# One engine issues every transfer: SyncE's transfers put into the program's own order in a gated mix of sliding-window attention and a GELU block

## The chip, the cores and the metric

The kernel runs on one core of a Trainium2 chip. A core has a matrix engine (TensorE; PE in the profile, with its weight loads listed apart as PEld), a vector engine (VectorE, DVE), a scalar engine (ScalarE, ACT), a general engine (GpSimd, POOL) and an engine that here does nothing but issue transfers (SyncE, SP). Each works through its own list of instructions from first to last; between engines there are semaphores. Transfers between the chip's memory and the on-chip memory are moved by 16 DMA engines. The metric is the device time of one execution in microseconds (us), the median of several runs.

## The reference

For x of 2048 tokens by 512, in fp32:

```python
g = sigmoid((x * gate_w).sum(-1, keepdims=True))
q, k, v = split(x @ wqkv)            # 32 heads of 16, per head 2048 x 16
scores = q k^T / 4, kept where 0 <= i - j < 256, else -1e9
a = softmax(scores) v @ wo
b = gelu(x @ w1 + b1) @ w2 + b2      # 512 -> 1792 -> 512
out = g * a + (1 - g) * b
```

## The kernel before, in words

**Dense work.** All large products (qkv, the two of the GELU block, and wo) are made from pairs: every fp32 operand is split into a high part and a low remainder, and one product is three matmuls (`mm3`, lines 92 to 95) of 128x128 weights on 128x512 moving data. Tokens are cut into four tiles of 512 (`T`). `dense()` is one long generator: `qkv(t)` for the four tiles, then eight turns `mlp(n)` over `TURNS` (half of the 1792 columns for one tile of tokens: first the "u" products and the GELU, then the "y" products), then `final(t)`, the product with wo and the mix.

**Attention.** Heads are taken in eight groups of four (`g_`), keys in 16 blocks of 128. For each block `att_max` multiplies queries by keys on a "dense" layout (tiles `qd` and `kd`, result `sm`, line 446) to find each row's maximum on VectorE; twelve blocks later (`LEAD`) `att_exp` makes the scores on another layout (`qs`, `ks`, result `st`, line 490), ScalarE takes the exponential and GpSimd cuts the window; `att_pvs` multiplies with the values in `vbuf` (line 527). q, k and v were written to device memory by `qkv` and are read back by `load_qd`, `load_kd`, `load_qs`, `load_ks` and `att_load_v`. A group's stretch of 512 tokens is one "slot", four blocks long, and `qd`, `kd`, `ks` have two slots: the next stretch is loaded while the present one is used, and it can't be written before the last products on the slot's old content have been made.

**What sets the order.** The main loop runs over blocks; in each of the four quarters of a block it emits the attention's products and then `fill`s in a share (`STEP / 4`, or `STEP0 / 4` for the first twelve) of the dense generator's matmuls. `START` is how much dense work is done before attention begins. Work of the other engines is put off by `after(ns, fn)` against a clock of the program's own, which counts matmuls; `tick` runs what has come due, and `need` runs events until a condition is met. The engines listed in `MANUAL` take their instructions in exactly the order in which this emits them. SyncE is not in that list before: its transfers are ordered by the framework's scheduler, which may move them past one another. In the built program all 749 transfers are on SyncE; eight semaphores are used in turn, so a transfer waits for the landing of the eighth before it.

**Around the change.** At the end of a block with `m % NB == (u >= 0)`, that is after the second block of each stretch, `load_qd` and `load_kd` ask for the next stretch. At the end of a turn's "u" products `load_x` asks for the next tile's x, four transfers of 512 KB (line 590), into the one buffer `xt`. `load` brings weights at a pace (`PACE`), and `split` cuts them into halves `LAND` later. `ya_load` fetches the addend of the "y" products. `att_norm` divides: it loads the denominators (565), writes the reciprocals back (570), loads numerators and spread reciprocals (575), multiplies and stores (580).

Of the kernel before, what the change touches and what calls it, by code (L numbers as in the profile page):

```python
# [32 lines left out]
def gated_mix(ctx: ExitStack, tc: tile.TileContext, x, wqkv, wo, w1, b1, w2, b2, gate_w, out):  # L33
# [11 lines left out]
    def f32(ap):  # L45
        return ap.bitcast(F32)
# [98 lines left out]
            nc.sync.dma_start(raw.rearrange("p (c f) -> p c f", c=NC) if len(src.shape) == 3 else raw, src)  # L145
        raws[key] = raw

    def split(key, eng):

        kind, i = key  # L150
        raw = raws.pop(key)
        w = sb.tile([128, 2, T], F32R, tag="w", bufs=14, name=f"{kind}_{i}")
        nc.scalar.activation(w[:, 0], raw, AF.Copy)
        wt[key] = w.rearrange("p s (c f) -> p s c f", c=NC) if kind in ("qk", "w1") else w

        def lo():
            eng.tensor_sub(w[:, 1], raw, f32(w[:, 0]))
            done.add(("w", key))
        after(700, lo)

    paced = [0.0]

    def load(key):

        paced[0] = max(now[0], paced[0] + PACE)
        after(paced[0] - now[0], load_now, key)

    def load_now(key):
        load_raw(key)
        after(LAND, split, key, nc.vector)  # L170

# [78 lines left out]
    def qkv_qk(t, j):  # L250

        xt = xts[t]
        dst, i = (SQ[t], j) if j < NC else (SK[t], j - NC)
        w = wt["qk", j]
        p = ps.tile([128, T], F32, tag="d", bufs=2, name=f"qk{t}_{j}")
        for c in range(NC):
            mm3(p, w[:, 0, c], w[:, 1, c], xt[:, c, 0], xt[:, c, 1], c == 0, c == NC - 1)
            yield MM3
        e = sb.tile([128, 2, T], F32R, tag="h", bufs=7, name=f"qke{t}_{j}")

        h = 1 if j < NC else 0

        def hi():
            nc.scalar.activation(e[:, h], p, AF.Copy)  # L264

        def lo():
            nc.vector.tensor_sub(e[:, 1 - h], p, f32(e[:, h]))  # L267

        def store():
            to = dst[:, :, :, i].rearrange("h d s c -> (h d) s c")  # L270
            nc.sync.dma_start(to[:, 0:2], f32(e))
            nc.sync.dma_start(to[:, 2], f32(e[:, h]))
            done.add(("qk", t, j))
        after(100, hi), after(700, lo), after(700 + HOLD, store)

    def qkv_v(t, b):
        xt = xts[t]
        p = ps.tile([128, D], F32, tag="d", bufs=2, name=f"v{t}_{b}")
        ts = slice(b * 128, (b + 1) * 128)
        for c in range(NC):  # L280
            w = wt["v", c]
            mm3(p, xt[:, c, 0, ts], xt[:, c, 1, ts], w[:, 0], w[:, 1], c == 0, c == NC - 1)
            yield MM3
        vx = f32(sb.tile([128, 2, T], F32R, tag="h", bufs=7, name=f"vx{t}_{b}"))
        vx = vx.rearrange("p s t -> p (s t)")[:, 0:H * 17].rearrange("p (h c) -> p h c", c=17)
        nc.gpsimd.memset(vx[:, :, 16:17], 1.0)

        def ev():
            to = vx[:, :, 0:16].rearrange("p (s i g a) d -> p i s g a d", i=2, s=2, a=2)
            by = p.rearrange("p (i a g s d) -> p i s g a d", i=2, a=2, s=2, d=16)  # L290
            for i in range(2):
                for s in range(2):
                    nc.scalar.activation(to[:, i, s], by[:, i, s], AF.Copy)
            after(HOLD, store)
# [17 lines left out]
    def qkv(t):  # L312
# [4 lines left out]
        if t == 0:  # L317
            keys = qk + [("v", c) for c in range(NC)]
            load_xr(0)
            for key in keys[0:4]:  # L320
                load_raw(key, True)
            warm(WARM[0])
            for b in range(NB):
                qkv_x(0, b)
            warm(WARM[1])
            split(keys[0], nc.vector)
            split(keys[1], nc.vector)
            nc.sync.dma_start(gwb, gate_w.partition_broadcast(128))
        need(*[("x", t, b) for b in range(NB)])
        for n, (kind, j) in enumerate(pieces):  # L330
            if not last and XAT <= n < XAT + NC:
                nc.sync.dma_start(XT[t][n - XAT], f32(xts[t][:, n - XAT]))
            if kind == "qk":
                need(("w", (kind, j)))
            else:
                need(*[("w", ("v", c)) for c in range(NC)])
            if t == 0 and n < 4:
                load_raw(keys[n + 4], True)
                load_raw(keys[n + 8], True)
            if t == 0 and n == 10:  # L340
                nc.sync.dma_start(b1c, b1.rearrange("(f p) -> p f", p=128))
            if kind == "qk":
                yield from qkv_qk(t, j)
            else:
                yield from qkv_v(t, j)
            if t == 1 and n % 3 == 2:
                clear_k(n // 3)
            if t == 2 and n < 4:
                clear_q(n)
            if t == 2 and n in (1, 2):  # L350
                load_kd(0, n - 1)
            if t == 2 and n in (8, 9):
                load_ks(0, n - 8)
            if t == 0:
                for i in ([2], [3], [4], [5], [6], [7, 8], [9, 10], [11])[n] if n < 8 else []:
                    split(keys[i], nc.vector if i % 2 else nc.gpsimd)
                if n == 1:
                    gate(0)
                    load_xr(1)
            elif n == 0 and not last:  # L360
                load_xr(t + 1)
            if last and n not in (6, 7):
                load(later.pop(0))
            if last and n == len(pieces) - 1:
# [196 lines left out]
    def att_norm(t, c):  # L561
# [5 lines left out]

        def rcp():
            nc.vector.reciprocal(den, den)
            nc.sync.dma_start(RD[t][c].rearrange("h (j c) -> (h j) c", c=32), den)  # L570

        def back():
# [4 lines left out]
        def mul():  # L577
            num, rb = tiles
            nc.vector.tensor_mul(num, num, rb)
            nc.sync.dma_start(OT[t][c], num)  # L580
            done.add(("o", t, c))
        after(6000, rcp), after(10500, back), after(17000, mul)


    w1k = w1.rearrange("(c p) f -> p c f", p=128)

    def load_x(t, name):
        xt = sb.tile([128, NC, 2, T], F32R, tag="xt", bufs=1, name=f"{name}{t}")
        for c in range(NC):
            nc.sync.dma_start(f32(xt[:, c]), XT[t][c])  # L590
        xts[t] = xt

    def load_o(t, cs=range(NC)):
# [58 lines left out]
    def ya_load(k):  # L652
# [7 lines left out]
        else:  # L660
            need(("y", 0, t, b))
            nc.sync.dma_start(ya, YA[t][slice(b * 128, (b + 1) * 128)])

    ybs = {}

    def mlp(n):
        half, t = TURNS[n]
        if n == 0:
            ya_load(0), ya_load(1)
        last = n % NT == NT - 1  # L670
        xt = xts[t]
        hs = []
        for i in range(HF):
# [13 lines left out]
            for c in range(NC):  # L687
                nc.sync.dma_start(XT[t][c], f32(xt[:, c]))
        if n + 1 < len(TURNS) and TURNS[n + 1][1] != t:
            load_x(TURNS[n + 1][1], f"mx{half}")  # L690
        ps_ = {}

        def y_start(b):
# [4 lines left out]
        def y_end(b):  # L698
# [7 lines left out]
            nc.vector.scalar_tensor_tensor(y, ps_[b], 0.5, yas.pop(n * NB + b), op0=ALU.mult, op1=ALU.add)  # L706
            ya_load(n * NB + b + 2)

            def store():
                nc.sync.dma_start((YA, YB)[half][t][ts], y)  # L710
# [40 lines left out]
    def final(t):  # L751
# [3 lines left out]
        for b in range(NB):  # L755
# [8 lines left out]
            for k in range(n):  # L764
# [8 lines left out]
                def ev(p=p, nb=nb, a=a, cs=cs):  # L773
                    need(("yb", nb))
                    nc.vector.scalar_tensor_tensor(a[:, cs], p, g[:, nb:nb + 1], a[:, cs],
                                                   op0=ALU.mult, op1=ALU.add)
                    nc.sync.dma_start(out[nb * 128:(nb + 1) * 128, cs], a[:, cs])
                after(100, ev)


    later = [("w1", i) for i in range(HF)] + [("w2", i) for i in range(HF)]
# [32 lines left out]
    for u in range(-LEAD, NU):  # L814
        m = u + LEAD
        gm, bm = divmod(m, NKB)
        step = STEP if u >= 0 else STEP0
        for i in range(4):
            for op in ORDER:
                if op == "s" and u >= 0:  # L820
                    att_exp(u // NKB, u % NKB, i)
# [9 lines left out]
            load_qs(0, m - QAT)  # L831
        if m == QAT + NT:
            load_qs(0, NT - 1)
        if m % NB == (u >= 0) and NB <= m < NU - NB:
            load_qd(*divmod(m // NB + 1, NT)), load_kd(*divmod(m // NB + 1, NT))
        if u % NB == 0 and NB <= u < NU - NB:
            load_ks(*divmod(u // NB + 1, NT))
        if u % NB == 2 and NB < u < NU - 3 * NB:
# [8 lines left out]
    tick(1e9)  # L847


MANUAL = {mybir.EngineType.PE, mybir.EngineType.Activation, mybir.EngineType.DVE, mybir.EngineType.Pool}  # L850
MM3 = 3 * 227
LASTN = 2
WARM = (7, 3)
RB = 4
NKB = S // 128
PTS = 14
RAWS = 122e3
PUT = 1200
LEAD = 12
QAT = 5  # L860
START = 90e3
NORM = 4500
YSWAP = 3
GELU = (700, 1500, 3600, 4600, 6000, 7000)
XAT = 3
ORDER = 'mspf'
XOR = 1
PACE = 5000.0
LAND = 10500.0
LANDO = 5000.0  # L870
HOLD = 1500.0
AHEAD = 9e3
STEP0 = 3000.0
PVAT = 2
STEP = 2422.0
_TC = dict()
_INS = ["A_x", "A_wqkv", "A_wo", "B_w1", "B_b1", "B_w2", "B_b2", "gate_w"]

# [17 lines left out]
```

## Time and profile before

| | before |
|---|---|
| median of 3 runs | 813.45 us (812.14 to 818.13) |
| profiled execution, its own time | 816.41 us |
| its span, first to last instruction | 814.7 us |
| TensorE busy | 755.1 us (93%) |
| VectorE / ScalarE / GpSimd busy | 511.1 / 432.2 / 425.6 us |
| DMA queue of SyncE | 174.90 MB, 80.3% of the 16 engines' span |
| mean granted TensorE clock | 0.969 |

How to read it: the profiled execution is one run, 3.0 us above the median. "Busy" for TensorE is modelled from pipelined matmuls. A matmul that runs at half the granted clock is as busy as one at the full clock, so time lost to the clock is not in the idle time. A row of the waits names who waited, for whom, how long in total, how many times and the longest. Rows of the timeline give start and duration in us; for SyncE the duration is that of issuing, not of the transfer. In the chain a transfer's row runs from its issue to its landing.

### The profile page before, as it was taken

The numbers are of one execution on the slowest core, as the hardware profiler recorded it, in microseconds if no ns is written. First come the engines' busy times: TensorE is split into PE (matmuls) and PEld (weight loads), VectorE is DVE, ScalarE is ACT, GpSimd is POOL, SyncE is SP. The second block draws the span as 40 slices with busy tenths as digits, with TensorE's granted clock in tenths as the row PEclk, the third lists the DMA queues.
The fourth block names the chain that finished last, engine by engine and source line by source line (L and its number), as shares of the span: only waits on it lengthen the run. The fifth ranks groups of instructions, "written<-read, shape, count | busy, mean of one in ns | idle before, by whom it ended". The sixth has DMA issues, their size and how long they took to land.

```text
span 814.7 us, 18155 instructions
## 1 busy us (share of the span) xinstructions
PE 755.1 (93%) x6102; PEld 618.5 (76%) x6102; DVE 511.1 (63%) x1548; ACT 432.2 (53%) x973; POOL 425.6 (52%) x1129
## 2 busy tenths in 40 slices
PE   8999999969599989997999898999989999989998
PEld 6888888747478867886887677778867887867776
DVE  4432358748556855794689577957855796663443
ACT  4434422448435843783487357636833774595631
POOL 3200002348546964785588466847954786685300
PEclk9999999979889999999999899999989999999999
DMA  9997999997867679887886797997688889676472
GB/s 291 399 283 287 351 285 300 284 196 202 244 163 172 129 232 220 208 195 180 209 171 155 191 237 184 245 214 146 166 216 203 195 226 211 158 192 199 153 247 104
DMA packets 203949, 176.06 MB, mean 216 GB/s; under 512 B 102480, under 2 KB 145744, under 8 KB 203856
## 3 DMA queue, kind: packets, MB, share of 16 engines
q1 hardware_dynamic: 203856, 174.90, 80.3%
q8 instruction: 48, 0.79, 0.5%
q14 instruction: 45, 0.37, 0.2%
HBM read 112.47 MB, written 62.39 MB: 215 GB/s over the span
## 4 chain that ended last, share of the span: by engine, by line
PE 53%; DMA 18%; DVE 5%; SPq 4%; issue 3%; ACT 3%; POOL 2%; POOLq 0%; DVEq 0%; ACTq 0%
DMA kd<-SK 9%; PE sm L446 6%; PE pv_sm L527 6%; PE st L490 6%; PE y L93 4%; PE u L93 4%; PE u L94 4%; PE u L95 4%; PE y L94 4%; PE y L95 4%; DVE jm L451 2%; PE a L93 2%; PE a L95 2%; PE a L94 2%; DMA vbuf<-SV 2%
## 5 line engine op out<-in xcount | busy, mean ns | idle before, releaser
L451 DVE CUSTOM_DVE_ANT_0 jm<-sm,mask 128x320 bf16<-128x320 f32 (+4 forms) x512 | 238.1, 465 | 122.2 <-PE sm L446 97.4
L505 ACT ACTIVATE pt<-st 128x320 f32<-128x320 f32 (+4 forms) x512 | 208.3, 425 | 194.0 <-PE st L490 190.1
L496 POOL TENSOR_SCALAR_AFFINE_SELECT pt<-pt 64x128 f32<-64x128 f32 x512 | 188.1, 367 | 206.7 <-ACT pt L505 186.5
L446 PE MATMUL sm<-kd,qd 96*128 96x320 f32 (+4 forms) x512 | 159.8, 314 | 47.3 <-DMA kd<-SK 26.8
L490 PE MATMUL st<-qs,ks 128*128 128x320 f32 (+4 forms) x512 | 159.4, 314 | 1.3 <-ACT pt L505 1.3
L446 PEld LDWEIGHTS sm<-kd,qd 96*128 96x128 f32 x512 | 98.5, 192 | 79.9 <-issue 45.3
L499 POOL TENSOR_SCALAR_AFFINE_SELECT pt<-pt 64x128 f32<-64x128 f32 x448 | 156.8, 350 | 0.0
L490 PEld LDWEIGHTS st<-qs,ks 128*128 128x128 f32 x512 | 99.9, 195 | 21.7 <-ACT pt L505 2.1
L473 POOL CAST qs<-tt 4x512 fp32r<-4x512 f32 x128 | 87.5, 684 | 38.6 <-DVE tt L467 19.3
L93 PE MATMUL y<-w,h 128*128 128x512 f32 x224 | 94.3, 421 | 0.0
L94 PE MATMUL y<-w,h 128*128 128x512 f32 x224 | 90.7, 405 | 0.0
L95 PE MATMUL y<-w,h 128*128 128x512 f32 x224 | 90.4, 404 | 0.0
L527 PE MATMUL pv_sm<-pt,vbuf 64*32 64x320 f32 (+4 forms) x1408 | 78.5, 360 | 2.6 <-POOL pt L496 1.7
L93 PE MATMUL u<-mx,w 128*128 128x512 f32 x196 | 79.3, 405 | 0.0
L527 PE MATMUL pv_st<-pt,vbuf 64*32 64x320 f32 (+4 forms) x1408 | 78.0, 360 | 1.3 <-POOL pt L496 1.1
L94 PE MATMUL u<-mx,w 128*128 128x512 f32 x196 | 78.0, 398 | 0.0
L95 PE MATMUL u<-mx,w 128*128 128x512 f32 x196 | 77.5, 395 | 0.0
L527 PEld LDWEIGHTS pv_sm<-pt,vbuf 64*32 64x32 f32 x1408 | 54.0, 111 | 23.6 <-issue 4.0
L95 PEld LDWEIGHTS y<-w,h 128*128 128x128 f32 x224 | 43.7, 195 | 10.8 <-DVE h L645 0.4
L527 PEld LDWEIGHTS pv_st<-pt,vbuf 64*32 64x32 f32 x1408 | 50.1, 111 | 1.7 <-POOL pt L496 1.4
L551 DVE TENSOR_TENSOR nd<-nd,pv_sm 128x512 f32<-128x512 f32 x32 | 21.9, 685 | 45.5 <-ACT nd L548 42.4
L267 DVE TENSOR_TENSOR qke<-qk,qke 128x512 fp32r<-128x512 f32 x32 | 22.1, 689 | 43.6 <-ACT qke L264 35.6
(140 smaller groups left out, 1328.2 us busy)
## 6 DMA issues: line engine op xcount, KB each, us to landing
kd<-SK SPq DMA_DIRECT2D x32, 384.0 KB
qd<-SQ SPq DMA_DIRECT2D x64, 192.0 KB
qs<-SQ SPq DMA_DIRECT2D x64, 192.0 KB
mx<-XT SPq DMA_DIRECT2D x24, 512.0 KB
SQ<-qke SPq DMA_DIRECT2D x16, 512.0 KB
SK<-qke SPq DMA_DIRECT2D x16, 512.0 KB
ND<-nd SPq DMA_DIRECT2D x32, 256.0 KB
raw_w<-in_B_w_dram SPq DMA_DIRECT2D x28, 256.0 KB
```

The costliest lines, as they stand in the source:

```text
L93: nc.tensor.matmul(p, lh, rh, start=first, stop=False)
L94: nc.tensor.matmul(p, lh, rl, start=False, stop=False)
L95: nc.tensor.matmul(p, ll, rh, start=False, stop=last)
L267: nc.vector.tensor_sub(e[:, 1 - h], p, f32(e[:, h]))
L446: nc.tensor.matmul(p[:, :w], qd[0:96, n, pr, 128 * j:128 * (j + 1)], kd[0:96, n, pr, k1 - w:k1], start=True, stop=True)
L451: nc.vector.tensor_tensor_reduce(junk[:, :w], p[:, :w], mask[:, 320 - w:320], 1.0, -3e38, ALU.add, ALU.max, M[:, 2 * (b % RB) + hb, pr:pr ...
L473: nc.gpsimd.tensor_copy(dst, tt[32 * i:32 * i + 4].unsqueeze(1).broadcast_to([4, 2, 2 * RB, 32]))
L490: nc.tensor.matmul(p[:, :w], ks[:, slot(g_, kb // NB), pr, at:at + 128], qs[:, pr, k0:k0 + w], start=True, stop=True)
L496: nc.gpsimd.affine_select(out=v[:, :, 0:64], in_=v[:, :, 0:64], pattern=[[0, 2], [1, 64]], compare_op=ALU.is_ge, fill=0.0, base=0, channel ...
L499: nc.gpsimd.affine_select(out=v[:, :, W:W + 64], in_=v[:, :, W:W + 64], pattern=[[0, 2], [-1, 64]], compare_op=ALU.is_ge, fill=0.0, base=- ...
L505: nc.scalar.activation(pt[:, pr, :w], p[:, :w], AF.Exp, scale=SCALE)
L527: nc.tensor.matmul(pv[r // 64][32 * i:32 * i + 32, q - c * T:e - c * T], vts[g_, b // NB][r:r + 64, v:v + 32], rhs(r), start=start, stop=s ...
```

## The change

SyncE is added to `MANUAL`, so transfers are issued in the order in which the program emits them, and the emission is changed to fit:

- Next keys and queries of the dense layout: both loads move from the end of the second block of a stretch to the end of the first quarter of its first block, the keys now ahead of the queries.
- Next x: the four 512 KB parts are emitted `MXAT` = 5500 ns of program time apart, and a turn on another tile waits in the emission for the last of them.
- Stores stand later: `HOLD` goes from 1500 to 4000 ns (attention results, y), q, k and v keep 1500 (`HOLDQ`), the output store gets 1200 of its own (`HOLDO`), and the division's stores become events of their own (`DIV`). The fetch of the next addend waits `HOLD` too.
- Weights: from 152 us of program time on (122 before) they use a pool of two buffers, with a count of free ones; `PACE` goes from 5000 to 4000 ns and `LAND` from 10500 to 7500. For the first tile all twelve weight loads are emitted at the start.
- Shares: `START` 90 to 105 us, `STEP0` 3000 to 2750, `STEP` 2422 to 2330 ns.

No instruction of arithmetic is added or taken away. The diff, cut:

```diff
+    slots = [0, 0]
     def load_now(key):
+        if now[0] >= RAWS:
+            if slots[0] - slots[1] == 2:
+                return after(500, load_now, key)
+            slots[0] += 1
+            after(LAND, split, key, nc.vector, True)
+        else:
+            after(LAND, split, key, nc.vector)
         load_raw(key)
-        after(LAND, split, key, nc.vector)
...
-        after(100, hi), after(700, lo), after(700 + HOLD, store)
+        after(100, hi), after(700, lo), after(700 + HOLDQ, store)
...
-            for key in keys[0:4]:
+            for key in keys:
                 load_raw(key, True)
...
-            if t == 0 and n < 4:
-                load_raw(keys[n + 4], True)
-                load_raw(keys[n + 8], True)
...
         def rcp():
             nc.vector.reciprocal(den, den)
+
+        def keep():
             nc.sync.dma_start(RD[t][c].rearrange("h (j c) -> (h j) c", c=32), den)
...
             nc.vector.tensor_mul(num, num, rb)
-            nc.sync.dma_start(OT[t][c], num)
+
+        def store():
+            nc.sync.dma_start(OT[t][c], tiles[0])
             done.add(("o", t, c))
-        after(6000, rcp), after(10500, back), after(17000, mul)
+        for ns, fn in zip(DIV, (rcp, keep, back, mul, store)):
+            after(ns, fn)
...
+        def part(c):
+            nc.sync.dma_start(f32(xt[:, c]), XT[t][c])
+            if c == NC - 1:
+                done.add(name)
         for c in range(NC):
-            nc.sync.dma_start(f32(xt[:, c]), XT[t][c])
+            after(MXAT * c, part, c)
...
+        if n and TURNS[n - 1][1] != t:
+            need(f"mx{n - 1}")
...
-            ya_load(n * NB + b + 2)
+            after(HOLD, ya_load, n * NB + b + 2)
...
-                    nc.sync.dma_start(out[nb * 128:(nb + 1) * 128, cs], a[:, cs])
-                after(100, ev)
+                def store(nb=nb, a=a, cs=cs):
+                    nc.sync.dma_start(out[nb * 128:(nb + 1) * 128, cs], a[:, cs])
+                after(100, ev), after(100 + HOLDO, store)
...
         for i in range(4):
+            if i == 1 and m % NB == 0 and NB <= m < NU - NB:
+                load_kd(*divmod(m // NB + 1, NT)), load_qd(*divmod(m // NB + 1, NT))
...
-        if m % NB == (u >= 0) and NB <= m < NU - NB:
-            load_qd(*divmod(m // NB + 1, NT)), load_kd(*divmod(m // NB + 1, NT))
...
-MANUAL = {mybir.EngineType.PE, mybir.EngineType.Activation, mybir.EngineType.DVE, mybir.EngineType.Pool}
+MANUAL = {mybir.EngineType.PE, mybir.EngineType.Activation, mybir.EngineType.DVE, mybir.EngineType.Pool,
+          mybir.EngineType.SP}
...
-RAWS = 122e3
+RAWS = 152000.0
-START = 90e3
+START = 105000.0
-PACE = 5000.0
-LAND = 10500.0
+PACE = 4000.0
+LAND = 7500.0
-HOLD = 1500.0
+HOLD = 4000.0
+HOLDQ = 1500.0
+HOLDO = 1200.0
+DIV = (6000, 9000, 12000, 18500, 22000)
+REST = 1000.0
+MXAT = 5500.0
-STEP0 = 3000.0
+STEP0 = 2750.0
-STEP = 2422.0
+STEP = 2330.0
```

More of the change, by code (lines that the diff above doesn't have):

```diff
@@ L146, in load_raw, with split @@
         raws[key] = raw
-    def split(key, eng):
+    def split(key, eng, slot=False):
         kind, i = key
@@ L158, in lo, with free @@
             done.add(("w", key))
+            if slot:
+                after(REST, free)
+        def free():
+            slots[1] += 1
         after(700, lo)
@@ L293, in ev @@
                     nc.scalar.activation(to[:, i, s], by[:, i, s], AF.Copy)
-            after(HOLD, store)
+            after(HOLDQ, store)
         def store():
@@ L662, in ya_load, with ya_of @@
             nc.sync.dma_start(ya, YA[t][slice(b * 128, (b + 1) * 128)])
+    def ya_of(k):
+        while k not in yas:
+            step_todo()
+        return yas.pop(k)
     ybs = {}
@@ L689, in mlp @@
         if n + 1 < len(TURNS) and TURNS[n + 1][1] != t:
-            load_x(TURNS[n + 1][1], f"mx{half}")
+            load_x(TURNS[n + 1][1], f"mx{n}")
         ps_ = {}
@@ L705, in y_end @@
                 y = ybs["w"][:, b]
-            nc.vector.scalar_tensor_tensor(y, ps_[b], 0.5, yas.pop(n * NB + b), op0=ALU.mult, op1=ALU.add)
-            ya_load(n * NB + b + 2)
+            nc.vector.scalar_tensor_tensor(y, ps_[b], 0.5, ya_of(n * NB + b), op0=ALU.mult, op1=ALU.add)
+            after(HOLD, ya_load, n * NB + b + 2)
             def store():
```

## The prediction

> **What bounds the kernel now.** I read the page's first two parts and its DMA queues, then the waits of TensorE, then SyncE's timeline and the chain around the longest of them.
>
> ```profile
> PE 755.1 (93%) x6102; PEld 618.5 (76%) x6102; DVE 511.1 (63%) x1548; ACT 432.2 (53%) x973; POOL 425.6 (52%) x1129
> ...
> PEclk9999999979889999999999899999989999999999
> ...
> q1 hardware_dynamic: 203856, 174.90, 80.3%
> q14 instruction: 45, 0.37, 0.2%
> ```
> ```profile
> core 0: 814.7 us, clock 0.969
> ```
>
> TensorE is busy for 755.1 of 814.7 us and no other engine comes near, so it is the bound. Two things can still be saved on it: its idle time, 814.7 - 755.1 = 59.6 us, and the time at a lower clock, (1 - 0.969) x 814.7 = 25.3 us. The same matmuls can't come below 814.7 - 59.6 - 25.3 = 729.8 us. The DMA engines, at 80.3%, are busy for 654 us: below that floor, but not by much.
>
> ```profile
> PE sm L446 <- DMA kd<-SK: 26.8, 11, 7.8
> PE sm L446 <- DMA vbuf<-SV: 9.7, 1, 9.7
> PE sm L446 <- DMA qs<-SQ: 4.0, 2, 2.9
> ...
> PE sm L446 <- DMA OT<-num: 1.7, 1, 1.7
> ```
>
> These rows of TensorE's waits name a transfer in the steady part. All end at line 446, the first product on a freshly loaded stretch; the row names the transfer that landed last, and what the product reads is kd and qd. Sum: 26.8 + 9.7 + 4.0 + 1.7 = 42.2 us, 71% of the idle time. The other 17.4 us are the start, the end and short waits for other engines.
>
> Why are kd and qd late? First SyncE's timeline at the longest wait, then rows of the chain:
>
> ```profile
> 210.12 1.74 SPq L590 DMA_DIRECT2D mx<-XT  x4
> 211.91 0.51 SPq L419 DMA_DIRECT2D qd<-SQ  x1
> 212.47 1.37 SPq L413 DMA_DIRECT2D kd<-SK  x2
> 213.88 0.85 SPq L432 DMA_DIRECT2D vbuf<-SV  x1
> ```
> ```profile
> 146.38 5.86 DMA kd<-SK
> 164.43 10.39 DMA kd<-SK
> 213.88 8.92 DMA vbuf<-SV
> 288.28 10.58 DMA kd<-SK
> 364.40 10.75 DMA kd<-SK
> 617.75 6.33 DMA kd<-SK
> 635.03 8.28 DMA kd<-SK
> 672.52 6.96 DMA kd<-SK
> ```
>
> The four mx transfers, 4 x 512 KB, go out right ahead of the second qd and of kd. In the chain a transfer takes 8.9 to 10.8 us to land at 213, 288 and 364, each just behind an x load, and 5.9 to 8.3 at 146 and after 600 (10.4 at 164, behind stores of the qkv stage).
>
> **The change part by part.** *Keys sooner.* The lead is counted in blocks.
>
> ```profile
> L446 PE MATMUL sm<-kd,qd x512: 193/311/607, 106.7 to 712.5; 96*128 96x320 f32 x150, 96*128 96x128 f32 x6, 96*128 96x64 f32 x5, 96*128 96x256 f32 x5
> L413 SPq DMA_DIRECT2D kd<-SK x56: 430/677/2666, 84.3 to 688.3; - x56
> ```
> ```profile
> L419 SPq DMA_DIRECT2D qd<-SQ x64: 303/464/2048, 98.9 to 685.6; - x64
> ```
>
> 512 products, four a block, run from 106.7 to 712.5: 605.8 / 128 = 4.73 us a block, and (605.8 - 42.2 - 25.3) / 128 = 4.2 us without the waits and the low clock. Before, kd is emitted two blocks ahead of its use: 9.5 us. Issuing two kd and two qd takes 2 x 0.68 + 2 x 0.46 = 2.3 us, and landing 5.9 to 10.8: 8.2 to 13.1 us are needed where 9.5 are there, so some stretches are late and some not. After, it is emitted 3.75 blocks ahead: 3.75 x 4.2 = 15.8 us against the same 8.2 to 13.1. The worst landing leaves 2.7 us, a usual one of 7 leaves 6.5. The slot is freed by the block just before, a quarter of a block ahead of the request, so at that point SyncE waits for little.
>
> *Next x in four parts.* With 5.5 us between them one 512 KB part stands ahead of a request, not four, and the landings near 10 us should fall to the 6 to 8 of the other rows. The exception is the first turn:
>
> ```profile
> 198.19 0.91 SPq L688 DMA_DIRECT2D XT<-xt  x2
> ...
> 202.39 0.43 SPq L688 DMA_DIRECT2D XT<-xt  x1
> ...
> 204.02 0.47 SPq L688 DMA_DIRECT2D XT<-xt  x1
> ```
>
> Four stores of the last x (XT) must land before the first part of the next can overwrite their source. Before, other transfers were let through between 198 and 210. After, SyncE stands at that part with vbuf and qs behind it, for about a landing of 6 us. A wait of some microseconds is likely to remain there.
>
> *The sum on the waits.* Of 42.2 us I let 37 go and keep 5, for the first turn and one or two crowded stretches.
>
> *The clock.* It is lost behind waits; four windows, with the share of DMA and GB/s after the clock:
>
> ```profile
> 223.00:233.00 10.00, 9.99 (x122) 7.62 (x123) 4.41 (x15) 2.79 (x6) 4.40 (x12) 0.73 0.56 133
> 528.00:532.00 4.00, 2.37 (x13) 1.75 (x12) 1.73 (x9) 0.96 (x3) 1.62 (x6) 1.00 1.14 188
> 532.00:540.00 8.00, 8.00 (x126) 6.39 (x125) 4.59 (x16) 3.12 (x7) 5.66 (x16) 1.00 0.90 191
> 624.00:628.00 4.00, 3.68 (x11) 3.17 (x12) 2.44 (x9) 0.88 (x2) 0.46 (x2) 0.57 0.50 175
> ```
>
> Behind the 9.7 us wait the clock is 0.73 for 10 us, a loss of 2.7. At 624, behind a wait of about 2 us, it is 0.57 for 4 us, a loss of 1.7; at 528 to 532, with 1.6 us idle, it stays at 1.00. So short waits cost clock sometimes. With 37 of 42.2 gone I let 21 of the 25.3 us go and keep 4. The Trainium skill ("TensorE: Matmul & The Clock Gate", Part 1) says that the clock falls after an idle window of about 3.4 us; by that rule the short waits that I keep would cost no clock, and the sum would be some 4 us lower. The row at 624 speaks against it, the one at 532 for it.
>
> *The division and the end.* The reciprocals' chain is stretched by `DIV` and `HOLD`: from the result's store to the product's store it was 1.5 + 4.5 + 17 = 23 us of program time and is 4 + 4.5 + 22 = 30.5. Inside the loop the products wait for `final` anyway. At the end they don't: the last two tiles' products are all that the last matmuls need.
>
> ```profile
> 314.85 4.36 DMA OT<-num
> ...
> 473.19 3.90 DMA RD<-den
> 477.11 6.20 DMA rb<-RD
> ```
> ```profile
> 790.53 0.23 PE a L93
> ```
>
> For the third tile the order of the built program puts the RD store behind the first store of `out`; from there 3.9 + 6.2 + 4.4 us of landings and about 4.4 for the reload, with some 3 us of arithmetic and issue, make 22. The two final tiles in between are 2 x 48 matmuls less the 12 that are done, at 0.23 us each: 84 x 0.23 = 19 us. I add 3 us; bounds: 0 if landings at the quiet end are short, and 7.5 if the whole stretch shows.
>
> *Shares.* `START` moves 15 us of dense matmuls ahead of attention, and 90 + 12 x 3.0 + 128 x 2.422 = 436.0 becomes 105 + 12 x 2.75 + 128 x 2.33 = 436.2: dense work still runs out with attention. A block carries 4% less of it, so the vector engines are asked for more per microsecond.
>
> ```profile
> 420.00:440.00 20.00, 18.49 (x174) 15.12 (x173) 19.04 (x52) 17.00 (x38) 18.67 (x42) 1.00 0.65 150
> 144.00:720.00 576.00, 527.47 (x4812) 433.48 (x4810) 401.89 (x1301) 330.30 (x738) 376.49 (x995) 0.96 0.81 197
> ```
>
> Over 144 to 720 VectorE is busy for 401.9 of 576 us (70%) and has room; while GELU runs, as at 420 to 440, it has 19.04 of 20, and TensorE idles 1.5 us. Some such stretches will lose a little more: I add 2 us, bounds 0 and 7 (a further 1 us in each of seven turns on GELU).
>
> *Weights.* `LAND` at 7.5 us instead of 10.5 puts ScalarE's copy closer to the load's issue.
>
> ```profile
> ACT w L153 <- DMA raw_w<-in_B_w_dram: 4.1, 2, 2.4
> ```
>
> It waited there for 4.1 us in all, and ScalarE has 47% of its time free: I cost it at nothing, hidden behind that idle time. If transfers go out late, it is the first place where ScalarE, and then the exponentials, stand: bound 28 loads x 1 us. Instructions are the same in number (749 transfers and 4662 matmuls in both built programs), so nothing else is added.
>
> *Sum*, on the profiled execution of 816.4 us: 816.4 - 37 - 21 + 3 + 2 = 763.4. The median of the runs lay 3.0 us below it (813.45), so 760.
>
> **The rivals.**
>
> *Gains halved by crowding* (789). In 144 to 720 the DMA engines are busy at 0.81; the same bytes in 58 us less are 0.81 x 576 / 518 = 0.90. If kd is in time but vbuf, qs and ks, now behind it, take over the role, half of the 58 us stay: 813.5 + 5 - 29 = 789. For it: the 9.7 us row names vbuf. Against it: they are needed 2 or more blocks after their request, as before.
>
> *Slower: a wait in front of everything* (835). In a fixed order a transfer that waits for its engine holds all that stand behind it. The waits of SyncE before:
>
> ```profile
> SPq L405 <- PE st L490: 35.5, 12, 7.4
> SPq L555 <- DVE nd L551: 34.2, 15, 5.8
> SPq L659 <- DVE yo L706: 29.2, 13, 8.4
> ```
>
> If a wait as long as the longest, 8.4 us, stands ahead of a kd with the slow landing, the lead of 15.8 is overdrawn by 8.4 - 2.7 = 5.7 us, and 2.7 of clock follow: 8.4 us a stretch. The 58 us that I let go are used up at 7 of the 31 stretches; at 10 it is 813.5 - 58 + 5 + 84 = 844, and with some of them half as long about 835. Against it: stores are emitted 4 us late, behind the point at which the result is made, and 15.8 us of lead swallow a first 2.7 to 6.5 us. The Trainium skill ("DMA: Bandwidth & Descriptors", the anatomy of one DMA) says that DMA engines never wait on semaphores and that each wait is sat out by the issuing sequencer before dispatch; by that rule this rival is the general case for an in-order queue. The three rows, in which it is SyncE that waits, agree.
>
> *It doesn't do what it says* (813). Eight semaphores in turn mean that a transfer waits for the eighth before it. If SyncE runs behind the program's clock all the time, kd is emitted sooner but issued no sooner. For it: DMA at 80.3%; against it: issue times of 0.4 to 0.7 us x 749 are at most some 500 us, and the idle gaps in SyncE's timeline.
>
> **How the numbers follow.** The forecast, 760, has 0.62, with a range of its own from 746 (816.4 - 42.2 - 25.3 - 3.0, every wait gone and nothing added) to 780 (12 us of waits and 8 of clock kept, 3.7 more at the end and in GELU stretches). Halved gains 0.16, no change 0.07, slower 0.15. One per cent is 8 us, about what a measurement of this kernel can tell from no change (the three runs lie 6 us apart). Faster by over 1% (below 805) is 0.62 + 0.16 = 0.78. The range runs from 742, a little below the best case since the median's distance from the profile is itself uncertain, to 810, which takes in the halved gains and leaves out the slower case and most of no change.
>
> **What would show it.** Right: at the first products of a stretch the waits for transfers sum to under 10 us; the mean clock is above 0.98; mx rows in SyncE's timeline stand singly, with kd ahead of qd; TensorE is above 96%. The first turn's XT stores are followed by SyncE's longest wait. Wrong: TensorE idles as long at line 446 with vbuf or qs named; ScalarE waits at line 153's copy for raw_w in many places; SyncE's waits on a result of VectorE stand just ahead of kd; or the last matmuls, on `a`, wait by more than 8 us for the division.

## The result, and the profile after

The changed kernel takes 783.68 us (782.26 to 788.64, four runs) against 812.80 us for the kernel before on the same chip: a ratio of 0.964, 95% interval [0.958, 0.971]. That is faster by 29 us where 53 were forecast. The profiled execution, at 788.64 us, is the slowest of the four; profile against profile the difference is 816.4 - 788.6 = 27.8 us.

The first parts of the page after, and its mean clock:

```profile
PE 747.3 (95%) x6102; PEld 616.2 (78%) x6102; DVE 510.5 (65%) x1548; ACT 432.9 (55%) x973; POOL 431.3 (55%) x1129
...
q1 hardware_dynamic: 203856, 174.90, 87.9%
```
```profile
core 0: 786.9 us, clock 0.985
```

TensorE's idle time is 786.9 - 747.3 = 39.6 us (59.6 before), the loss to the clock by its mean 0.015 x 786.9 = 11.8 (25.3). These two overlap, because the clock is also low while TensorE waits. In this window of the kernel before, TensorE is idle from 213.3 us on (the 9.7 us wait that ends at 223.0):

```profile
211.00:223.00 12.00, 2.30 (x13) 1.71 (x12) 3.73 (x11) 2.13 (x5) 4.31 (x12) 0.80 1.06 275
```

The clock of 0.80 makes 0.20 x 12 = 2.4 us of loss by the mean, and all of it falls into the wait: the trace has the clock at half from 218.2 us on. Added up over both traces, the loss while TensorE is busy is 19.6 us before and 9.8 after; 6.0 and 2.2 more fall into idle time. So of the 27.8 us, 20.0 come from idle time and 9.8 from the clock, and 2.0 are given back in a busy time that is modelled and holds the same matmuls.

TensorE's waits after, in us: total, times, longest:

```profile
PE st L500 <- ACT pt L515: 7.0, 4, 5.5
PE sm L456 <- DMA ya<-in_B_b_dram: 4.9, 1, 4.9
PE pv_st L537 <- POOL pt L506: 3.9, 2, 3.4
PE pv_sm L537 <- DVE M L461: 3.8, 6, 0.9
PE a L93 <- DVE ao L802: 3.5, 2, 2.0
...
PE sm L456 <- DMA qd<-SQ: 0.4, 1, 0.4
```

And the rows of before that answer to the first, third, fourth and fifth:

```profile
PE st L490 <- ACT pt L505: 1.3, 1, 1.3
PE pv_st L527 <- POOL pt L496: 1.1, 2, 0.7
PE a L93 <- DVE ao L775: 1.1, 1, 1.1
...
PE pv_sm L527 <- DVE M L451: 0.5, 1, 0.5
```

At the first product (line 456 now) the named transfers went from 42.2 us to 4.9 + 0.4 = 5.3, and the 4.9, as shown below, is not a late key or query. The waits for other engines went the other way. With the last matmuls' 3.5 - 1.1 = 2.4 us set apart, TensorE's idle time that names no transfer at line 446 or 456 was 59.6 - 42.2 - 1.1 = 16.3 and is 39.6 - 5.3 - 3.5 = 30.8: 14.5 us more.

Windows of the steady part (busy time of TensorE, its weight loads, VectorE, ScalarE, GpSimd; granted clock; DMA share; GB/s):

```profile
190.00:300.00 110.00, 109.14 (x1093) 91.45 (x1093) 81.58 (x278) 65.75 (x148) 84.67 (x232) 1.00 0.96 221
300.00:660.00 360.00, 349.11 (x3380) 292.03 (x3386) 276.92 (x905) 223.42 (x505) 266.37 (x697) 1.00 0.96 213
```

For 470 us TensorE is busy for 97 to 99% at a clock that rounds to 1.00 (3.4 us at half clock, at 310, are in it), with the DMA engines at 0.96. What is left lies around that stretch, in two places above all. The first, at 164 us, in the timelines of SyncE, ScalarE, VectorE and TensorE (start, duration, instruction, in brackets the idle time before it and what ended it):

```profile
159.17 1.95 SPq L145 DMA_DIRECT2D raw_w<-in_B_w_dram  x1
...
167.69 0.63 ACT L153 ACTIVATE w<-raw_w 128x512 fp32r<-128x512 f32 x1 [7.79 <-DMA raw_w<-in_B_w_dram]
...
168.36 0.69 DVE L157 TENSOR_TENSOR w<-raw_w,w 128x512 fp32r<-128x512 f32 x1 [5.74 <-ACT w L153]
...
169.51 0.64 PE L456 MATMUL sm<-kd,qd 96*128 96x320 f32 x1 [4.94 <-DMA ya<-in_B_b_dram]
```

TensorE's row names ya, but read upwards the cause is a weight. It was issued at 159.17 and landed by 167.7, 8.5 us later. ScalarE stood 7.8 us for it, VectorE 5.7 for ScalarE, and TensorE 4.9 for the maxima queued on VectorE behind that subtraction. The second place, at 711 us:

```profile
688.19 0.47 SPq L412 DMA_DIRECT2D ks<-SK  x1
700.16 0.34 SPq L565 DMA_DIRECT2D ND<-nd  x1
...
704.93 2.07 SPq L629 DMA_DIRECT2D or<-OT  x3
...
714.22 2.07 ACT L632 ACTIVATE ot<-or 128x512 fp32r<-128x512 f32 x3 [5.06 <-DMA or<-OT]
```

SyncE issues nothing from 688.7 to 700.2, where a store waits for its result; the reload of OT for the product with wo, which could have gone, is issued behind it at 704.93, and ScalarE stands 5.1 us for it with the exponentials queued behind. TensorE idles 5.5 of its 7.0 us there.

Three more rows of the waits of all engines (before: 12.4, 4.1 and 3.8 us):

```profile
ACT ot L632 <- DMA or<-OT: 26.1, 8, 8.8
ACT w L153 <- DMA raw_w<-in_B_w_dram: 23.5, 9, 7.8
DVE num L591 <- DMA rb<-RD: 21.0, 10, 4.3
```

### The profile page after: what moved, and what is told of

The parts are those of the page before. It is cut to its first block, busy times and chain, and to the rows that moved or that the text cites. A ratio compares the mean times of both kernels' runs of the same rounds, so it can differ in the third digit from the quotient of the medians.

```text
span 786.9 us, 18205 instructions
## 1 busy us (share of the span) xinstructions
PE 747.3 (95%) x6102; PEld 616.2 (78%) x6102; DVE 510.5 (65%) x1548; ACT 432.9 (55%) x973; POOL 431.3 (55%) x1129
## 5 line engine op out<-in xcount | busy, mean ns | idle before, releaser
L506 POOL TENSOR_SCALAR_AFFINE_SELECT pt<-pt 64x128 f32<-64x128 f32 x512 | 182.6, 357 | 153.7 <-ACT pt L515 131.9
L509 POOL TENSOR_SCALAR_AFFINE_SELECT pt<-pt 64x128 f32<-64x128 f32 x448 | 167.3, 373 | 0.0
L456 PE MATMUL sm<-kd,qd 96*128 96x320 f32 (+4 forms) x512 | 157.3, 310 | 9.9 <-DMA ya<-in_B_b_dram 4.9
L500 PE MATMUL st<-qs,ks 128*128 128x320 f32 (+4 forms) x512 | 156.1, 309 | 7.0 <-ACT pt L515 7.0
L500 PEld LDWEIGHTS st<-qs,ks 128*128 128x128 f32 x512 | 97.8, 191 | 27.4 <-ACT pt L515 8.7
L93 PE MATMUL y<-w,h 128*128 128x512 f32 x224 | 90.7, 405 | 0.0
L94 PE MATMUL y<-w,h 128*128 128x512 f32 x224 | 88.6, 395 | 0.0
L95 PE MATMUL y<-w,h 128*128 128x512 f32 x224 | 88.3, 394 | 0.0
L537 PE MATMUL pv_sm<-pt,vbuf 64*32 64x320 f32 (+4 forms) x1408 | 82.5, 366 | 5.6 <-DVE M L461 3.5
L537 PE MATMUL pv_st<-pt,vbuf 64*32 64x320 f32 (+4 forms) x1408 | 80.9, 366 | 6.7 <-POOL pt L506 3.9
L537 PEld LDWEIGHTS pv_sm<-pt,vbuf 64*32 64x32 f32 x1408 | 60.0, 112 | 23.7 <-DVE M L461 6.3
L537 PEld LDWEIGHTS pv_st<-pt,vbuf 64*32 64x32 f32 x1408 | 54.1, 112 | 7.6 <-POOL pt L506 4.2
L299 POOL MEMSET vx<- 128x32 f32 x16 | 2.5, 156 | 93.1 <-DMA SK<-qke 32.0
```

The costliest lines, as they stand in the source:

```text
L93: nc.tensor.matmul(p, lh, rh, start=first, stop=False)
L94: nc.tensor.matmul(p, lh, rl, start=False, stop=False)
L95: nc.tensor.matmul(p, ll, rh, start=False, stop=last)
L456: nc.tensor.matmul(p[:, :w], qd[0:96, n, pr, 128 * j:128 * (j + 1)], kd[0:96, n, pr, k1 - w:k1], start=True, stop=True)
L500: nc.tensor.matmul(p[:, :w], ks[:, slot(g_, kb // NB), pr, at:at + 128], qs[:, pr, k0:k0 + w], start=True, stop=True)
L506: nc.gpsimd.affine_select(out=v[:, :, 0:64], in_=v[:, :, 0:64], pattern=[[0, 2], [1, 64]], compare_op=ALU.is_ge, fill=0.0, base=0, channel ...
```

## The experiments

Each kernel ran beside the kernel before on the same chip; ratios are to it, with a 95% interval. Differences between two changed kernels are taken between medians, some from different chips, on which the kernel before has medians from 811.0 to 815.7 us: such a difference is uncertain by a few us. Theories are named in each expectation.

### Is it the lead?

The changed kernel with the old places for the request:

```diff
-            if i == 1 and m % NB == 0 and NB <= m < NU - NB:
-                load_kd(*divmod(m // NB + 1, NT)), load_qd(*divmod(m // NB + 1, NT))
...
+        if m % NB == (u >= 0) and NB <= m < NU - NB:
+            load_kd(*divmod(m // NB + 1, NT)), load_qd(*divmod(m // NB + 1, NT))
```

> The kernel after, with keys and queries of the dense layout asked for at the old place, after the second block of a stretch (keys still first). Theory A (the lead is what removed the waits): the lead falls from 3.75 to 2 blocks, 8.7 us against 8.2 to 13 needed; 800 to 810 us, waits for transfers at the first product of a stretch back to 20 to 40 us. Theory B (the fixed order alone keeps kd in front): 783 to 788 us.

Measured: 813.94 us, ratio 1.003 [1.000, 1.006], theory A's wait and 4 us more than its band. Its longest wait of TensorE:

```profile
PE sm L456 <- DMA qd<-SQ: 24.5, 7, 7.6
```

Without the earlier request nothing of the gain is left, and the waits at the first product are back under the name of qd, which now is asked for last. The reverse, the kernel before with the new places alone and its transfers still ordered by the scheduler:

> The kernel before, with one edit: keys and queries of the dense layout are asked for at the change's place, keys first; the scheduler still orders SyncE, x comes in one piece, shares and holds are the old ones. Theory A (the lead is the gain, and the scheduler keeps to it): waits for transfers at the first product of a stretch fall from 42 to under 15 us, 780 to 792 us. Theory B (the edits need each other; the scheduler puts kd behind the x loads again): 800 to 812 us.

Measured: 789.73 us, ratio 0.971 [0.965, 0.978]. This one edit brings 2.9 of the 3.6%, as theory A has it. In its waits kd is gone and another row has grown:

```profile
PE sm L446 <- DVE M L451: 12.7, 13, 4.2
```

Then the parts of x, all four at once again in the changed kernel:

```diff
-MXAT = 5500.0
+MXAT = 0.0
```

> The kernel after, with the four parts of the next x emitted together. Theory A (with 15.8 us of lead a landing of 10.8 us behind an x load is still in time): 784 to 788 us, waits at the first product of a stretch under 10 us. Theory B (an x load in one piece still makes kd late three to six times by 4 us and costs the clock behind it): 795 to 805 us.

Measured: 796.99 us, ratio 0.984 [0.978, 0.989]: the time of theory B, but not by way of kd. The parts are worth some 13 us by the medians:

```profile
PE pv_sm L537 <- DVE M L461: 9.5, 6, 5.3
...
PE sm L456 <- DVE M L461: 9.5, 5, 6.6
...
PE pv_st L537 <- DMA vbuf<-SV: 4.1, 1, 4.1
```

With the longer lead kd survives the four parts in a row: no transfer is named at line 456. What is late are transfers with less slack: vbuf at 212 us, behind the first x load, and the reciprocals at 354, behind the third, for which VectorE stands 5.9 us and TensorE 5.3. The 6.6 us stand at 170, before the first x load at 203; the edit doesn't reach that wait, which is 4.9 us in the changed kernel.

### What does the fixed order cost?

The kernel before with SyncE in the program's order and nothing else:

```diff
-MANUAL = {mybir.EngineType.PE, mybir.EngineType.Activation, mybir.EngineType.DVE, mybir.EngineType.Pool}
+MANUAL = {mybir.EngineType.PE, mybir.EngineType.Activation, mybir.EngineType.DVE, mybir.EngineType.Pool,
+          mybir.EngineType.SP}
```

> The kernel before, with the one edit that SyncE takes its transfers in the program's order; requests, stores and shares stay as before. Theory A (a store 1.5 us behind its result makes SyncE wait in front of everything, and kd keeps its two blocks of lead): 815 to 840 us, SyncE's waits on VectorE in front of kd longer than before. Theory B (the order alone brings most of the gain, by keeping kd from being put behind others): 785 to 800 us.

Measured: 859.54 us, ratio 1.059 [1.054, 1.063]: the sign of the slower theory, and more than its band. Waits of TensorE and of SyncE:

```profile
PE sm L446 <- DMA kd<-SK: 66.9, 17, 15.1
...
SPq L659 <- DVE yo L706: 37.1, 10, 9.2
```

The same edit on top of the earlier request:

> The kernel before with two edits: kd and qd asked for at the new place, and SyncE in the program's order; stores, x and the division as they were. Theory A: the later stores and the parts of x are what makes the fixed order bearable, so without them kd is late again behind waits for VectorE, though by less than with the old lead: 800 to 830, with kd or vbuf named at the first product for 20 us or more. Theory B: the lead alone carries the fixed order: 786 to 796, as with the scheduler.

Measured: 814.27 us, ratio 0.999 [0.996, 1.003]; the fixed order costs 814.3 - 789.7 = 24.5 us here, by medians from two chips. The time is in the band of theory A, but kd is not what is late. The longest waits of TensorE are these, and behind the first of them stands this row of VectorE:

```profile
PE sm L446 <- DVE M L451: 22.6, 16, 7.5
PE pv_st L527 <- DMA vbuf<-SV: 18.8, 4, 9.8
```
```profile
603.91 0.69 DVE L579 TENSOR_TENSOR num<-num,rb 128x512 f32<-128x512 f32 x1 [8.60 <-DMA rb<-RD]
```

VectorE stands 8.6 us for the reciprocals that are read back, and the maxima behind it hold TensorE for 7.5. Then the changed kernel with its stores back at their old distance:

```diff
-HOLD = 4000.0
+HOLD = 1500.0
...
-HOLDO = 1200.0
+HOLDO = 0.0
```

> The changed kernel with its stores of the division's terms and of YA and YB, and the reload of YA, at the old 1.5 us behind their results instead of 4 us, and the stores of out at 0 instead of 1.2; the order is SyncE's fixed one, kd, qd and x stand at the new places. Theory A: the later places of the stores make the fixed order bearable. With the old places it costs about 24 us, as it does on the old kernel with early keys (814.3 against 789.7), in place of 6: 796 to 808, with SyncE's waits on VectorE (nd, yo) at 40 us or more and a transfer or the copy of the maxima named at the first products. Theory B: the parts of x and the division's places carry it, and the stores' places are worth little: 784 to 790, SyncE's waits on nd and yo under 25 us.

Measured: 790.33 us, ratio 0.971 [0.964, 0.978], at the upper edge of B's band, while SyncE's waits on nd and yo are as A has them: 21.5 + 14.2 + 10.6 = 46.3 us, where the same three rows of the changed kernel sum to 9.7.

```profile
SPq L565 <- DVE nd L561: 21.5, 8, 10.0
...
SPq L682 <- DVE yo L733: 14.2, 8, 3.8
...
SPq L679 <- DVE yo L733: 10.6, 5, 3.0
```

By the medians the later stores are worth about 7 us (the intervals overlap a little), so neither theory holds alone: SyncE can stand for 46 us and most of it costs nothing. What else brings the price of the fixed order from 24.5 us down to the 6 of the next run isn't told apart here: the parts of x, the division's places, the weights and the shares are left. Of the edits undone alone the parts cost the most. Last, the changed kernel with SyncE given back to the scheduler, all else kept:

```diff
-MANUAL = {mybir.EngineType.PE, mybir.EngineType.Activation, mybir.EngineType.DVE, mybir.EngineType.Pool,
-          mybir.EngineType.SP}
+MANUAL = {mybir.EngineType.PE, mybir.EngineType.Activation, mybir.EngineType.DVE, mybir.EngineType.Pool}
```

> The kernel after, with SyncE handed back to the scheduler; all else of the change is kept. Theory A (the order and the early request need each other: the scheduler moves kd behind other transfers again): 800 to 812 us, with waits for kd at line 456 of 20 us or more. Theory B (asking sooner is enough, the order is not what counts): 780 to 790 us, waits for kd under 8 us.

Measured: 777.54 us (772.59 to 782.15), ratio 0.956 [0.950, 0.962]. Theory A falls, and it came out even below B's band: 6 us better than the changed kernel by the medians, though the two intervals overlap. The fixed order isn't what brings the gain; by the medians it costs some, which these runs don't settle. Its timeline of SyncE at the end shows where:

```profile
693.28 1.24 SPq L629 DMA_DIRECT2D or<-OT  x2
...
701.36 0.33 SPq L565 DMA_DIRECT2D ND<-nd  x1
```

The reload of OT goes 8 us ahead of the store that it stood behind at 700, and TensorE's wait for the exponentials, 7.0 us, is 2.7 in this kernel.

### The waits that are left

A longer distance from a weight's load to its copy, in the changed kernel:

```diff
-LAND = 7500.0
+LAND = 10500.0
```

> The kernel after, with ScalarE's copy of a loaded weight (and of the first tile of the attention's result) put back to 10.5 us behind its request, from 7.5. Theory A (late loads hold ScalarE's list, VectorE behind it and TensorE behind that: 4.9 us and a low clock at 164, 5.5 us and a low clock at 711): the 7.8 us wait of ScalarE for a weight at 160 goes, 770 to 778 us. Theory B (what is left is the closer packing of attention, ScalarE's waits are not on the path): 781 to 788 us.

Measured: 790.34 us, ratio 0.973 [0.966, 0.979]; theory A falls, and the time lies 2 us above B's band. From ScalarE's wait and those of TensorE:

```profile
ACT w L153 <- DMA raw_w<-in_B_w_dram: 8.9, 4, 6.1
...
PE y L93 <- ACT w L153: 5.0, 1, 5.0
PE sm L456 <- DMA qd<-SQ: 4.8, 1, 4.8
```

ScalarE's wait falls from 23.5 to 8.9 us, as it should, but now a "y" product at 483 us waits for a weight that is split too late, and at 163 qd is late where the weight was. The same edit with the scheduler's order:

> The kernel after, with both: SyncE ordered by the scheduler and the copies 10.5 us behind the request. Theory A (two causes at two places: the fixed order costs at the end, the early copies at 164): 766 to 774 us, 5 to 9 us under the run with the scheduler alone (777.5). Theory B (the scheduler already lets late loads through, so the copies' place matters no more): 775 to 779 us.

Measured: 782.57 us (775.65 to 784.56), ratio 0.961 [0.953, 0.969], above both bands and no better than with 7.5 us. The wait at 164 shrinks to 1.8 us, and the one on the "y" product is there with 4.9. The old shares of dense work in the changed kernel (`START` 90 us, `STEP0` 3000, `STEP` 2422):

> The kernel after, with the old shares: START 90 us, STEP0 3000, STEP 2422 ns. Theory A (a closer packing of attention is what VectorE, ScalarE and GpSimd can't follow: some 20 us of TensorE's waits name them): these waits fall by 5 to 10 us, but attention starts 15 us sooner in the crowded stage of qkv; 778 to 786 us. Theory B (the new shares carry part of the gain): 790 to 800 us, with new waits before 200 us.

Measured: 788.57 us, ratio 0.972 [0.964, 0.980], between the bands, with an interval that overlaps that of the changed kernel. Undoing the shares gains nothing: TensorE's idle time is 786.0 - 744.3 = 41.7 us, and by the medians it costs 5 us, where I had the new shares cost 2. The division's products later, for all tiles but a turn's last:

```diff
-        for ns, fn in zip(DIV, (rcp, keep, back, mul, store)):
+        for ns, fn in zip(DIV if c == NC - 1 else DIVL, (rcp, keep, back, mul, store)):
...
+DIVL = (6000, 9000, 12000, 22500, 25500)
```

> The changed kernel with the products of the division later for all tiles but the last of a turn (product 22.5 us and store 25.5 us of program time behind the result instead of what they were; reciprocal and its reload at 6 to 12). Theory A: VectorE standing for the reloaded reciprocals (rb, 21.0 us in ten waits after the change) is what lets TensorE's short waits of 0.4 to 1.4 us grow, so with it gone TensorE's named waits for VectorE fall and 4 to 9 us come back: 774 to 780. Theory B: VectorE's idle time there is off the path; 782 to 786, with the row of rb smaller and TensorE's idle time the same.

Measured: 785.85 us, ratio 0.966 [0.961, 0.970]: theory B. VectorE's row is halved,

```profile
DVE num L591 <- DMA rb<-RD: 10.5, 4, 3.6
```

and TensorE's idle time, 783.8 - 743.6 = 40.2 us, is what it was. The short waits of the attention's products for VectorE's maxima (3.8 us) are gone, but those of the first products grew from 2.5 to 5.1, and the wait at 164 from 4.9 to 6.4.

### A version that is better than both

Three edits at once: the scheduler's order, the later products, and 10.5 us for the weights ahead of the two-buffer pool alone, where the wait at 164 stood.

```diff
-            after(LAND, split, key, nc.vector)
+            after(LANDE, split, key, nc.vector)
...
+LANDE = 10500.0
```

> The changed kernel with three edits together: SyncE's order back to the scheduler, the later products of the division, and a longer distance from load to copy (10.5 us) for the weights ahead of the first raw slot limit alone, where the wait at 164 stood. Theory A: the three waits are separate, so their gains add: about 6 us from the order, 3 to 5 from the copy, 3 to 6 from the products: 764 to 772. Theory B: each wait that goes lets the next one stand in its place: 776 to 784.

Measured: 775.26 us (769.44 to 776.16), ratio 0.950 [0.944, 0.956], an interval that lies wholly below that of the changed kernel. From its page:

```profile
PE 744.9 (96%) x6102; PEld 613.7 (79%) x6102; DVE 511.1 (66%) x1548; ACT 430.4 (56%) x973; POOL 427.7 (55%) x1129
```

The span is 773.0 us, so TensorE's idle time is 28.1 where the changed kernel has 39.6. The three rows of ScalarE and VectorE that sum to 70.6 us in the changed kernel (ot, w, rb) sum to 21.5 here. By size the time lies between the theories: 8.4 us are gained of the 12 to 17 that theory A's three terms add up to. Its distance to the scheduler's order alone is 2.3 us by the medians, and the two intervals overlap, so what the other two edits bring in it is not settled.

## Why the prediction was right and wrong, step by step

**Keys sooner: right, and the main thing.** Of the waits at the first product 37 us were to go and 36.9 went. That the two agree so closely is luck: by cause all but 0.4 us of the waits for keys and queries went, and the 4.9 us under the name of ya belong to the weights. The 5 us that I kept, for the first turn and crowded stretches, didn't come. A block takes

```profile
L456 PE MATMUL sm<-kd,qd x512: 193/311/636, 121.9 to 671.9; 96*128 96x320 f32 x150, 96*128 96x128 f32 x6, 96*128 96x64 f32 x5, 96*128 96x256 f32 x5
```

(671.9 - 121.9) / 128 = 4.30 us and not 4.2, so the lead is 16.1 us. Both reversals bear it out: without the request's new place 0 of the gain is left, and by itself it gives 26 us. "SyncE waits for little" at the request was wrong, though what TensorE waits for transfers at the first products is 5.3 us all the same. Three rows of SyncE's waits after:

```profile
SPq L423 <- PE st L500: 29.4, 17, 6.4
...
SPq L565 <- DVE den L579: 11.7, 1, 11.7
...
SPq L606 <- DMA XT<-xt: 6.1, 2, 4.9
```

**Next x in four parts: right in sign, wrong in its reason.** mx rows do stand singly now, with kd ahead of qd:

```profile
203.07 0.42 SPq L606 DMA_DIRECT2D mx<-XT  x1
203.55 0.92 SPq L436 DMA_DIRECT2D qs<-SQ  x2
204.51 0.93 SPq L423 DMA_DIRECT2D kd<-SK  x2
205.48 1.20 SPq L429 DMA_DIRECT2D qd<-SQ  x2
```

But the landings that were to fall to 6 to 8 us didn't. From the semaphore events of the two traces I work out, for the loads of kd after 150 us, a median of 6.7 us and 10.8 at most before, and 6.2 and 11.8 after. The parts don't make kd faster; undone, they make vbuf and VectorE's reloads late. The exception I made for the first turn was wrong too: SyncE does stand 4.9 us at the XT stores, but its longest wait is the 11.7 us at 688 (for nd; the row names den, which VectorE started as nd ended), and TensorE is busy for 109.1 us of the 110 from 190 on.

**The clock: 21 forecast, 13.5 measured by the mean, 9.8 while TensorE is busy.** Long waits took their clock with them, as reckoned, but the sum took the low clock within a wait off twice, once with the wait and once with the clock. That is 6.0 of the 25.3 us, so only 19.6 were there to be gained beside the idle time, and the floor of 729.8 is too low by about as much. The 11.8 us that are left, where I kept 4, lie around waits that I hadn't forecast: the granted clock is at half from 167, 310, 692 and 716 us on, for 3.4 or 6.8 us each. Windows behind two of them (the second with the idle stretch ahead of it), and a group of short waits with the window behind it:

```profile
166.00:174.00 8.00, 4.49 (x13) 3.92 (x14) 5.22 (x17) 4.70 (x9) 0.00 (x0) 0.57 0.88 320
308.00:310.00 2.00, 0.65 (x5) 0.22 (x3) 1.97 (x8) 0.52 (x1) 0.00 (x0) 1.00 1.01 323
310.00:314.00 4.00, 3.40 (x78) 2.81 (x86) 3.48 (x8) 2.19 (x6) 2.92 (x6) 0.57 1.11 197
450.00:458.00 8.00, 6.51 (x116) 5.02 (x114) 6.80 (x19) 4.15 (x10) 4.76 (x8) 1.00 0.90 223
458.00:462.00 4.00, 3.67 (x19) 2.83 (x18) 3.57 (x12) 3.40 (x9) 3.58 (x10) 1.00 1.14 263
```

At 308 some 1.4 of 2 us are idle and the clock of the next 4 us is 0.57; at 450 about 1.5 us are idle within 8 and it stays at 1.00. The Trainium skill ("TensorE: Matmul & The Clock Gate", Part 1) puts the fall behind an idle window of about 3.4 us. If that window has to be idle from end to end, neither fall fits: at 308 the waits are short, and in the wait that ends at 169.5 TensorE stops at 164.6 and the clock falls at 167.0, 2.4 us later.

**Division and end: right in size, by another way.** 3 us forecast, 2.4 measured (`a` waits 3.5 us, before 1.1). I had the last products wait for the division's result itself. In the trace both waits, at 754 and 761, end with VectorE's reading of a finished product (`ao`), and VectorE stood ahead of it for the reciprocals, 2.1 us up to 750.0 and 2.6 up to 760.0. That the sizes agree is luck.

**Shares and the vector engines: the term that was mis-sized.** I added 2 us, bounds 0 and 7. Measured, the waits for other engines rose by 14.5 us, and 2.0 more show as busy time. The new shares are not the reason, since undoing them gained nothing. The step that failed is the one ahead of it, where I asked only how busy VectorE is and not for what it, or ScalarE, stands in its own order: the copy of a weight, the reload of the reciprocals and that of OT are waits inside the queues of the engines that also make the maxima and the exponentials. Those three rows went from 20.3 us to 70.6. The timelines at 164 and 711 show how two of them reach TensorE. But TensorE's idle time doesn't simply follow their sum: 45.2 us of them stand beside 34.5 of idle time with the scheduler's order alone, 28.5 beside 38.7 with the longer distance added, 21.5 beside 28.1 with all three edits. In the changed kernel the later products and the longer distance, each alone, shortened a row and brought no time back. So how much of the 14.5 us is due to which row isn't shown. In the prediction's sum the waits for transfers stand only at TensorE's own reads.

**Weights: wrong.** I costed `LAND` at nothing. The prediction did name line 153's copy as the first place to stand if transfers go out late, with ScalarE's free time as its cover. The cover failed at 164, where VectorE's subtraction waits for that copy: 4.9 us of TensorE, and about 2.1 of clock behind it (half of the 4.3 us that TensorE is busy until the clock is back at 173.8). Copies that wait in many places were one of the prediction's own signs of being wrong, and there are nine. The bound of 1 us a load was no bound: one of nine waits was 7.8. The longer distance doesn't mend it for free either, by the "y" product's wait in both kernels that have it.

**The rivals.** "A wait in front of everything" is a real mechanism. Alone on the kernel before it gives 859.5 us, more than my 835, with 37.1 us on one store of VectorE's results. In the changed kernel I found it to reach TensorE in one place, the store at 700 that holds OT. Of what I said against it the longer lead is shown: with it alone 24.5 us of the price of 48.5 are left, with the rest about 6. What the later stores add, about 7 us, isn't settled. "Gains halved by crowding" has nearly the right time, 789, for the wrong reason: the DMA share over 144 to 720 rose from 0.81 to 0.91, as estimated (0.90), but vbuf, qs and ks didn't take over.

**The sum.** In the terms of the prediction, profile against profile, -37 - 21 + 3 + 2 = -53 became -36.9 - 9.8 + 2.4 + 14.5 + 2.0 = -27.8. Nearly all that is missing lies in the clock and in the waits for other engines. The range that I gave the forecast itself ends too high by its own terms: 12 us of waits and 8 of clock kept, with 3.7 more, make 775 and not 780. The measured 784 lies above both.

**What stays open.** The 2.0 us of busy time that aren't matmuls at a lower clock; in the kernel with the old request, whose idle time is about that of before, the busy time less the clock's loss within it is 735.8, where the kernel before has 735.5 and the changed one 737.5. And the wait of 3.4 us at 690, where TensorE waits for GpSimd's cuts of the window in the last blocks, which have no maxima any more; nothing was tried for it. The nd whose store holds SyncE until 700 is made from the products behind this wait, so it may have a part in the wait at 711 too.

## What to carry to other kernels

Ask for a late load sooner before changing who orders the transfers: the request's place alone gave 26 of 29 us here, and it took the price of the fixed order from 48 us to 24; with the rest of the change about 6 are left. When the main wait goes, look at every instruction of the other engines that reads a transfer, and count what is queued behind it on that engine; a wait of ScalarE for a weight reached TensorE through VectorE, under the name of a transfer that had nothing to do with it.

## What the runs showed that I had not expected

With the DMA engines at 0.96 for 470 us TensorE still ran at 97 to 99%, so a high DMA share alone was no bound. The landings of kd were no shorter after the change than before it; only the slack ahead of them was longer. And one and the same edit, SyncE in the program's order, cost 48.5 us on the kernel before (859.5 against 811.0 on the same chip), 24.5 with the earlier request and about 6 on the changed kernel (an overlap of the intervals leaves the last open), so its price belongs to the order that it fixes.
